# Attention, a dense layer and routed experts on one Trainium2 core: fourteen subtractions of the first dense unit moved from VectorE to GpSimd, one activation moved up

## The chip, the cores and the metric

The kernel runs on one core of one Trainium2 chip. The metric is the device time of one execution in microseconds; smaller is better. Before the change, three runs took 1003.2, 1003.36 and 1005.94 us, a median of 1003.36 us.

## What is computed

Attention with a learned bias over positions feeds a dense two-layer block, whose result feeds eight experts of which each token takes one:

```
x = attention(q, k, v, bias)            # 2304 tokens x 512
h = x @ w_in                            # 512 x 2048
g = h - tanh(h)
y = g @ w_out                           # 2048 x 512
e = argmax(y @ w_gate)                  # one of 8 experts per token
out = gate * (relu(y @ w1[e]) @ w2[e])
```

Only the dense block (the middle three lines) is touched by the change.

## The kernel before, in words

All matrix products of the dense block are made from pairs of numbers. Each operand is kept as a high part (rounded) and a low part (the value less its high part), and every product is three matmuls: high by high, high by low, low by high. ScalarE writes the high part (a copy with rounding), and VectorE the low part (a subtraction of the high part from the value, both in SBUF).

The dense block walks over six units of 384 tokens (`Moe1`, `u` from 0 to 5). In a unit, each of 16 blocks `m` of the hidden layer goes through

- `l1(u, m)`: 12 matmuls of 128x384 (line 795) into one of two PSUM buffers `h`;
- `act(u, m)`: g = h - tanh(h), where tanh(h) is near h by a polynomial. ScalarE makes `z`, `t`, `mk` and `v` (lines 807, 808, 810, 811, 812), VectorE makes `w` from them (lines 813, 814, 817, 818, 819). Lines 813 and 814 read `h` from PSUM; 814 is the last reader of that buffer, so that `l1` of block m+2 waits for it. Lines 817, 818 and 819 read SBUF alone. There is one mask buffer `mk`: line 810 of a block waits for line 819 of the block before;
- `split_g(u, m)`: high part `gh` on ScalarE (line 825), low part `gl` on VectorE (line 826), both from SBUF;
- `l2(u, m)`: 9 matmuls of 128x512 (line 839) into three accumulators `y`, three steps after `l1`.

The order on each engine is the order of the program text, which the function `experts` writes step by step (step `i` is block `m` of a unit): `l1` of block i, `l2` of block i-3, then `stage.at`, then `act` of block i, then `split_g` of block i-1.

`stage.at` is where weights and tokens are brought in. Of the 32 weight blocks (16 of the first layer, "which" 0, and 16 of the second, "which" 1), 14 are split during attention by `high_w`; the other 18 are brought in during the first dense unit: `w_job` loads a block into one of four buffers `raw` (line 741, SP's queue) and `split_w` makes its high part (line 747, ScalarE) and its low part (line 749, VectorE). Ten of those 18 are of the second layer (blocks 6 to 15), eight of the first (blocks 8 to 15). They come at steps 1 (two), 2, 3, 4, 5 (two), 6, 7, 8, 9 (two), 10, 11, 12, 13 (two) and 14. In the same buffers come the four pieces of the next unit's tokens (`x_job`, at steps 7, 9, 11 and 13): the load, a scaling on GpSimd (line 774), the high part on ScalarE (line 779) and the low part on VectorE (line 783). A buffer `raw` is free for the load of the fourth job behind it once the low part is made.

Of the kernel before, what the change touches and what calls it, by code (L numbers as in the profile page):

```python
# [17 lines left out]
ALU = mybir.AluOpType  # L18
# [12 lines left out]
def r32(ap):  # L31
    return ap.bitcast(F32R)
# [656 lines left out]
class Moe1:  # L689
# [52 lines left out]

        return load, lambda: self.split_w(which, m, st.pop("raw"))

    def high_w(self, which, m, raw):
        nc, t = self.tc.nc, self.weights.tile(f"w{which}_{m}")
        nc.scalar.activation(r32(t[:, 0, :]), raw, AF.Copy)
        (self.win, self.wout)[which][m] = t
        return lambda: nc.vector.tensor_tensor(r32(t[:, 1, :]), raw, t[:, 0, :], op=ALU.subtract)

    def split_w(self, which, m, raw):
        self.high_w(which, m, raw)()

    def x_tiles(self, u):

# [3 lines left out]
    def x_job(self, u, k):  # L759
        nc, n, st = self.tc.nc, self.N, {}  # L760

        def load():
            st["raw"] = self.stage.raw(f"xf{u}_{k}")
            st["r"] = self.weights.first.tile([128, n], F32, name=f"xr{u}_{k}", tag="xr", bufs=2)
            t = slice(n * u, n * u + n)
            nc.sync.dma_start(st["raw"][:, 0:n], self.xt_d[128 * k : 128 * k + 128, t])
            for b in range(n * u // S, (n * u + n - 1) // S + 1):
                a, z = max(n * u, S * b), min(n * u + n, S * b + S)
                for j in range(2):
                    r = self.r_d[k, b, j : j + 1, a - S * b : z - S * b].to_broadcast([64, z - a])  # L770
                    nc.sync.dma_start(st["r"][64 * j : 64 * j + 64, a - n * u : z - n * u], r)

        def scale():
            nc.gpsimd.tensor_tensor(st["raw"][:, 0:n], st["raw"][:, 0:n], st.pop("r"), op=ALU.mult)

        def high():
            if k == 0:
                self.x[u] = self.x_tiles(u)
            nc.scalar.activation(r32(self.x[u][0][:, k, :]), st["raw"][:, 0:n], AF.Copy)

        def low():
            h, l = self.x[u]
            nc.vector.tensor_tensor(r32(l[:, k, :]), st.pop("raw")[:, 0:n], h[:, k, :], op=ALU.subtract)

        return load, scale, high, low

# [605 lines left out]
def experts(moe1, moe2, router, stage):  # L1392

    tc = moe2.tc
    nc = tc.nc
    nu, ns = Moe1.NU, 2 * (EARLY + FIXED)
    e0 = 16 * nu  # L1400
    items = [("m", u, m) for u in range(nu) for m in range(16)]
    items += [("e", s, f) for s in range(ns) for f in range(8)]
    first = {"m": moe1.l1, "e": moe2.l1}
    act = {"m": moe1.act, "e": moe2.act}
    second = {"m": moe1.l2, "e": moe2.l2}
    plan = {}

    def at(i, f, *a):
        plan.setdefault(i, []).append(lambda: f(*a))

    routed = [16 * u + 15 + LAG + (12 if u + 1 < nu else 10) for u in range(nu)]
    known = []
    for k in range(EARLY):
        i = routed[nu - 1 - EARLY + k] + 1 + 2 * k
        at(i, router.early, k)
        at(i + 2, moe2.early_regs, k)
        known.append(i + 3)
    i = routed[-1] + 1
    for j, f in enumerate(router.table()):
        at(i + j - 1, f)  # L1420
    for k in range(FIXED):
        at(i + 3, moe2.table_regs, EARLY + k, k)
        known.append(i + 4)
    at(i + 3, moe2.table_regs, ("s", 0), FIXED)
    for s in range(ns):
        b = e0 + 8 * s
        at(max(known[s // 2], b - 15), moe2.ids, s)
        for t in range(3):
            at(max(known[s // 2] + 2, b - 12), moe2.gather, s, t)
            at(b - 8 + t, moe2.x_in, s, t)  # L1430
            if s < ns - 1:
                at(b + 8 + LAG + t, moe2.out_t, s, t)
            else:
                at(b + 8 + LAG, moe2.out_t, s, t, ("tr", "y0", "y1")[t])
    for p in range(ns // 2):
        b = e0 + 16 * p
        for n in range(16):
            stage.add(START + max(known[p] + 3, b - 10) + (9 * n) // 10, START + max(known[p], b - 16), *moe2.w_job(p, n))
    b = e0 + 8 * ns
    at(b + LAG, moe2.small_l2, 0)  # L1440
    at(b - 20, moe2.small_ids, 0)
    for n in range(8):
        at(b - 16 + n, moe2.small_w, 0, n)
    at(b - 6, moe2.small_gather, 0)
    at(b - 2, moe2.small_x, 0)
    at(b - 1, moe2.small_l1, 0)
    at(b + 1, moe2.small_t, 0)

    split = None
    for i in range(len(items) + LAG):  # L1450
        if i < len(items):
            kind, *a = items[i]
            if i > 1:
                first[kind](*a)
        if i >= LAG:
            y, *b = items[i - LAG]
            second[y](*b)
            if y == "m" and b[1] == 15:
                for d, f in enumerate(router.unit(b[0], [moe1.acc.pop((b[0], t)) for t in range(3)])):
                    if f:  # L1460
                        at(i + 1 + d, f)
            elif y == "e" and b[1] == 7:
                moe2.y_out(b[0])
        if i < 2:
            moe1.split_g(0, i)
        stage.at(START + i)
        if 1 < i < len(items):
            act[kind](*a)
        if split:
            moe1.split_g(*split)  # L1470
        split = a if 1 < i < len(items) and kind == "m" else None
        for f in plan.pop(i, ()):
            f()
    for i in sorted(plan):
        for f in plan[i]:
            f()

    rest = nc.values_load(router.tab[0:1, 2 * NTAB : 2 * NTAB + 1], min_val=0, max_val=NREST)
    with tc.For_i(0, rest) as k:
        moe2.listed_regs(EARLY + FIXED, k + FIXED + 1)  # L1480
        moe2.pair(EARLY + FIXED)
# [3 lines left out]
def attention_moe(ctx, tc, q, k, v, moe_w_in, moe_w_out, w_gate, e_w1, e_w2, rows, dist, out):  # L1485
# [74 lines left out]
    router.open(pool, psum)  # L1560
    moe2 = Moe2(tc, pool, stage, moe1, psum, e_w1, e_w2, x2_d, list_d, out, router, ident)
    experts(moe1, moe2, router, stage)


# [35 lines left out]
```

## Time and profile before

| | |
|---|---|
| median of three runs | 1003.36 us |
| the profiled execution | 1004.94 us |
| its span, first to last instruction | 1003.1 us |
| TensorE busy (matmul) | 971.5 us, 97% |
| VectorE busy | 760.0 us, 76% |
| ScalarE busy | 633.2 us, 63% |
| GpSimd busy | 355.5 us, 35% |

The profiled execution is one run, 1.58 us above the median; 1.84 us of it lie outside the span. Busy shares are means over stages: the first dense unit, in which all that is changed lies, takes the span from 334 to 402 us, and its own rows have to be read. In the rows below, PE is TensorE's matmul, PEld its weight load, DVE is VectorE, ACT ScalarE, POOL GpSimd and SPq the queue of DMA issues on SyncE.

### The profile page before, as it was taken

Reading aid. Unit: us, or ns where it says so; the run is one execution under the profiler, and the core shown is the slowest. Engines: PE = TensorE matmul, PEld = TensorE weight load, DVE = VectorE, ACT = ScalarE, POOL = GpSimd, SP = SyncE. Lnnn points to the kernel's source line nnn. Section 1 sums busy time; section 2 is a strip of 40 time slices with the busy share of each in tenths; the row PEclk is TensorE's granted clock in tenths of the full one; section 3 lists DMA queues with packets and bytes.
Section 4 is the critical chain, followed back from the end, with each engine's and each line's share of the span. In section 5 each row is a group of like instructions: output and inputs, shape, how many; then the busy total and the mean of one; then the engine's idle time right before and its main releaser. Section 6 shows DMA issues by size and latency. Waiting matters only on the chain.

```text
span 1003.1 us, 20010 instructions
## 1 busy us (share of the span) xinstructions
PE 971.5 (97%) x7091; PEld 818.4 (82%) x7091; DVE 760.0 (76%) x1739; ACT 633.2 (63%) x1469; POOL 355.5 (35%) x338
## 2 busy tenths in 40 slices
PE   7799999999999999999999999999999999999996
PEld 3467766666676798889888889888889999999995
DVE  8996788989989799889889888988896454434321
ACT  7797778778777788756666665666875433434321
POOL 9682889788788000100201101101121142222101
PEclk9999999999999999999999999999999999999999
DMA  8676586966954232300300300202223244433601
GB/s 245 210 196 204 158 225 181 254 180 162 260 165 135 73 99 84 94 3 1 95 1 1 95 1 13 84 1 74 67 77 106 86 116 140 131 112 122 212 19 35
DMA packets 112796, 113.28 MB, mean 113 GB/s; under 512 B 61795, under 2 KB 79715, under 8 KB 112692
## 3 DMA queue, kind: packets, MB, share of 16 engines
q1 hardware_dynamic: 107684, 99.96, 34.2%
q0 software_dynamic: 4864, 11.89, 3.8%
q8 instruction: 58, 0.95, 0.4%
q14 instruction: 46, 0.38, 0.1%
q10 hardware_dynamic: 144, 0.11, 0.0%
HBM read 81.90 MB, written 30.08 MB: 112 GB/s over the span
## 4 chain that ended last, share of the span: by engine, by line
PE 65%; DVE 14%; issue 10%; DMA 5%; ACT 3%; POOL 1%; SPq 1%; POOLq 0%; DVEq 0%; ACTq 0%
PE y L839 17%; PE h L795 17%; PE eh L1233 6%; PE ey L1255 6%; DVE p L306 4%; PE s L286 4%; PE px L380 4%; DVE hid L101 2%; PE pv L412 2%; PE bps L116 2%; DMA out<-o,id 2%; PE pv L439 2%; DVE pt L384 1%; PE tr L966 1%; DVE wc L633 1%
## 5 line engine op out<-in xcount | busy, mean ns | idle before, releaser
L795 PE MATMUL h<-xh,w 128*128 128x384 f32 x768 | 215.2, 341 | 2.1 <-DVE t L814 2.1
L839 PE MATMUL y<-w,gh 128*128 128x512 f32 x576 | 179.9, 393 | 0.0
L795 PEld LDWEIGHTS h<-xh,w 128*128 128x128 f32 x768 | 140.4, 188 | 8.3 <-DVE t L814 2.8
L320 ACT ACTIVATE p<-p,nm 128x576 f32<-128x576 f32 x144 | 111.3, 773 | 34.2 <-DVE nm L306 33.9
L795 PE MATMUL h<-xl,w 128*128 128x384 f32 x384 | 129.0, 336 | 0.0
L839 PEld LDWEIGHTS y<-w,gh 128*128 128x128 f32 x576 | 106.8, 188 | 17.1
L306 DVE CUSTOM_DVE_ANT_0 p<-s,bias 128x576 f32<-128x576 f32 x144 | 103.6, 751 | 19.8 <-PE s L286 18.3
L1233 PE MATMUL eh<-xh,ew 128*128 128x288 f32 x512 | 116.5, 303 | 0.0
L839 PE MATMUL y<-w,gl 128*128 128x512 f32 x288 | 113.8, 395 | 0.0
L1255 PE MATMUL ey<-ehh,ew 128*128 128x288 f32 x512 | 112.3, 295 | 0.0
L1243 DVE SCALAR_TENSOR_TENSOR ehl<-eh,ehh 128x288 fp32r<-128x288 f32 x64 | 29.2, 456 | 109.1 <-ACT ehh L1242 109.1
L1242 ACT ACTIVATE ehh<-eh 128x288 fp32r<-128x288 f32 x64 | 26.2, 410 | 124.2 <-PE ey L1255 122.9
L807 ACT ACTIVATE z<-h 128x384 f32<-128x384 f32 x96 | 46.5, 484 | 75.3 <-PE h L795 75.3
L1233 PEld LDWEIGHTS eh<-xh,ew 128*128 128x128 f32 x512 | 85.9, 189 | 0.3 <-issue 0.2
L380 PE MATMUL px<-ident,p 128*128 128x128 f32 x576 | 80.1, 281 | 6.2 <-DVE pt L384 2.8
L1255 PEld LDWEIGHTS ey<-ehh,ew 128*128 128x128 f32 x512 | 85.7, 189 | 0.4 <-issue 0.4
L380 PEld LDWEIGHTS px<-ident,p 128*128 128x128 f32 x576 | 62.0, 141 | 29.0 <-issue 12.5
L1272 POOL DMA_INDIRECT out<-o,id x24 | 22.9, 954 | 154.8 <-ACT o L1289 131.3
L1233 PE MATMUL eh<-xl,ew 128*128 128x288 f32 x256 | 75.6, 295 | 0.0
L1255 PE MATMUL ey<-ehl,ew 128*128 128x288 f32 x256 | 75.5, 295 | 0.0
L813 DVE SCALAR_TENSOR_TENSOR w<-z,h 128x384 f32<-128x384 f32 x96 | 53.0, 552 | 28.9 <-ACT t L808 26.3
L795 PEld LDWEIGHTS h<-xl,w 128*128 128x128 f32 x384 | 72.3, 188 | 2.4
(487 smaller groups left out, 2364.3 us busy)
## 6 DMA issues: line engine op xcount, KB each, us to landing
rw<-in_moe_w SPq DMA_DIRECT2D x64, 256.0 KB, 2.9
bias_d<-bo SPq DMA_DIRECT2D x36, 295.5 KB, 4.0
w<-in_moe_w_out SPq DMA_DIRECT2D x16, 512.0 KB, 3.6
w<-in_moe_w_in SPq DMA_DIRECT2D x16, 512.0 KB, 4.4
bias<-bias_d SPq DMA_DIRECT2D x16, 288.0 KB, 3.9
w_d<-wc SPq DMA_DIRECT2D x18, 256.0 KB, 2.6
xf<-xt_d SPq DMA_DIRECT2D x24, 192.0 KB, 5.1
raw<-w_d SPq DMA_DIRECT2D x18, 256.0 KB, 3.7
```

Of the source, the lines that this page charges most:

```text
L286: nc.tensor.matmul(ps[w][:, c, 0:288], r32(q[r, a, 128 * i : 128 * i + 128] if i < 4 else self.tails(u)[:, a, :]), r32(k[r, b, kc : kc + 2 ...
L306: nc.vector.tensor_tensor_reduce(st["p"][:, c].rearrange("p (a x) -> p a x", a=2), st["ps", w][:, :, 0:288], bias[:, c].rearrange("p (a x) ...
L320: nc.scalar.activation(p[:, c], p[:, c], AF.Exp, bias=nm[:, w : w + 1], scale=-1.0, accum_out=self.st[us[0], "sm"][:, x : x + 1])
L380: nc.tensor.transpose(ps[:, 128 * j : 128 * j + 128], p[:, 128 * n : 128 * n + 128], self.ident)
L795: nc.tensor.matmul(ps[:, 0 : self.N], a, r32(b[:, k, :]), start=k + i == 0, stop=k == 3 and i == 2)
L807: nc.scalar.activation(z, h, AF.Square)
L813: nc.vector.scalar_tensor_tensor(w, z, self.C4, h, op0=ALU.mult, op1=ALU.mult)
L839: nc.tensor.matmul(self.acc[u, t], r32(a[:, c]), r32(w[:, b, :]), start=m + i == 0, stop=m == 15 and i == 2)
L1233: nc.tensor.matmul(ps[:, 0:SLOT], a, r32(b[:, k, 0:SLOT]), start=k + i == 0, stop=k == 3 and i == 2)
L1242: nc.scalar.activation(r32(h), ps[:, 0:SLOT], AF.Relu)
L1243: nc.vector.scalar_tensor_tensor(r32(l), ps[:, 0:SLOT], 0.0, h, op0=ALU.max, op1=ALU.subtract)
L1255: nc.tensor.matmul(st["y", d][:, 0:SLOT], a, r32(b), start=f + i == 0, stop=f == 7 and i == 2)
```

## The change

Three edits. The low part of a second-layer weight block that is brought in by `split_w` is made on GpSimd (the 14 blocks that `high_w` makes during attention stay on VectorE, and so do the eight first-layer blocks). The low part of each of the four token pieces of unit 1 is made on GpSimd; the pieces of all other units stay. At step 2, `act` stands ahead of `stage.at`.

```diff
-    def high_w(self, which, m, raw):
+    def high_w(self, which, m, raw, low=None):
         nc, t = self.tc.nc, self.weights.tile(f"w{which}_{m}")
         nc.scalar.activation(r32(t[:, 0, :]), raw, AF.Copy)
         (self.win, self.wout)[which][m] = t
-        return lambda: nc.vector.tensor_tensor(r32(t[:, 1, :]), raw, t[:, 0, :], op=ALU.subtract)
+        return lambda: (low or nc.vector).tensor_tensor(r32(t[:, 1, :]), raw, t[:, 0, :], op=ALU.subtract)
 
     def split_w(self, which, m, raw):
-        self.high_w(which, m, raw)()
+        self.high_w(which, m, raw, self.tc.nc.gpsimd if which else None)()
...
         def low():
             h, l = self.x[u]
-            nc.vector.tensor_tensor(r32(l[:, k, :]), st.pop("raw")[:, 0:n], h[:, k, :], op=ALU.subtract)
+            e = nc.gpsimd if u == 1 else nc.vector
+            e.tensor_tensor(r32(l[:, k, :]), st.pop("raw")[:, 0:n], h[:, k, :], op=ALU.subtract)
...
         if i < 2:
             moe1.split_g(0, i)
+        if i == 2:
+            act[kind](*a)
         stage.at(START + i)
-        if 1 < i < len(items):
+        if 2 < i < len(items):
             act[kind](*a)
```

Below, numbers at the end of a name count buffers; `w_6` to `w_15` beside `raw` are weight blocks, `w_2_...` beside `z` and `v` is the activation of block 2.

VectorE at steps 1 to 3, before the change:

```order
L826 TENSOR_TENSOR gl_0_5299<-w_0_5241,gh_0_5298 128x384
L826 TENSOR_TENSOR gl_1_5303<-w_1_5262,gh_1_5302 128x384
L749 TENSOR_TENSOR w_6_5306<-raw_5087,w_6_5306 128x512
L749 TENSOR_TENSOR w_8_5309<-raw_5089,w_8_5309 128x512
L749 TENSOR_TENSOR w_7_5329<-raw_5091,w_7_5329 128x512
L813 SCALAR_TENSOR_TENSOR w_2_5337<-z_2_5334,h_2_5316 128x384
L814 TENSOR_TENSOR t_2_5336<-h_2_5316,t_2_5336 128x384
L817 SCALAR_TENSOR_TENSOR v_2_5335<-z_2_5334,v_2_5335 128x384
L818 SCALAR_TENSOR_TENSOR w_2_5337<-v_2_5335,w_2_5337 128x384
L819 COPY_PREDICATED w_2_5337<-mk_2_5338,t_2_5336 128x384
L749 TENSOR_TENSOR w_9_5374<-raw_5093,w_9_5374 128x512
```

The same place with the change (lines from 814 on stand one or more further down in the new text):

```order
L827 TENSOR_TENSOR gl_0_5299<-w_0_5241,gh_0_5298 128x384
L827 TENSOR_TENSOR gl_1_5303<-w_1_5262,gh_1_5302 128x384
L749 TENSOR_TENSOR w_8_5309<-raw_5089,w_8_5309 128x512
L814 SCALAR_TENSOR_TENSOR w_2_5332<-z_2_5329,h_2_5316 128x384
L815 TENSOR_TENSOR t_2_5331<-h_2_5316,t_2_5331 128x384
L818 SCALAR_TENSOR_TENSOR v_2_5330<-z_2_5329,v_2_5330 128x384
L819 SCALAR_TENSOR_TENSOR w_2_5332<-v_2_5330,w_2_5332 128x384
L820 COPY_PREDICATED w_2_5332<-mk_2_5333,t_2_5331 128x384
L749 TENSOR_TENSOR w_9_5374<-raw_5093,w_9_5374 128x512
```

Two of three weight subtractions ahead of the activation of block 2 are gone from VectorE; the one of the first-layer block 8 (step 1) still stands ahead of it, since the activation was moved past the split of step 2 alone.

GpSimd through the unit, as a piece of the difference (lines with + are new; line 784 is the old 783):

```order
 L734 MEMSET cst 128x1
+L749 TENSOR_TENSOR w_6_5306<-raw_5087,w_6_5306 128x512
+L749 TENSOR_TENSOR w_7_5344<-raw_5091,w_7_5344 128x512
+L749 TENSOR_TENSOR w_8_5420<-raw_5312,w_8_5420 128x512
+L749 TENSOR_TENSOR w_9_5469<-raw_5347,w_9_5469 128x512
 L774 TENSOR_TENSOR xf_0_5472<-xf_0_5472,xr_0_5473 128x384
+L749 TENSOR_TENSOR w_10_5569<-raw_5423,w_10_5569 128x512
+L784 TENSOR_TENSOR xl_5573<-xf_0_5472,xh_5572 128x384
 L774 TENSOR_TENSOR xf_1_5578<-xf_1_5578,xr_1_5579 128x384
+L749 TENSOR_TENSOR w_11_5673<-raw_5526,w_11_5673 128x512
+L784 TENSOR_TENSOR xl_5573<-xf_1_5578,xh_5572 128x384
 L774 TENSOR_TENSOR xf_2_5683<-xf_2_5683,xr_2_5684 128x384
```

GpSimd had four instructions of any length in this unit, the scalings of line 774; now it has eighteen, and each low part of a token piece stands ahead of the next piece's scaling in its queue.

## Rows read from the trace of the kernel before

**Rows 1.** The page: span, and busy time of each engine.
```profile
span 1003.1 us, 20010 instructions
PE 971.5 (97%) x7091; PEld 818.4 (82%) x7091; DVE 760.0 (76%) x1739; ACT 633.2 (63%) x1469; POOL 355.5 (35%) x338
```
**Rows 2.** Chain that ended last, in order of time: start us, us, work.
```profile
402.40 2.08 PE h L795 x12
...
406.58 2.08 PE h L795 x12
...
753.45 2.08 PE y L839 x9
```
**Rows 3.** Timeline of PE, 345 to 403 us: start, us, instruction, [idle before <-releaser].
```profile
349.94 0.45 PE L795 MATMUL h<-xh,w 128*128 128x384 f32 x1 [0.88 <-DVE t L814]
...
380.06 0.44 PE L795 MATMUL h<-xh,w 128*128 128x384 f32 x1 [0.58 <-DVE t L814]
...
397.98 0.42 PE L795 MATMUL h<-xh,w 128*128 128x384 f32 x1 [0.65 <-DVE t L814]
...
402.24 0.34 PE L795 MATMUL h<-xh,w 128*128 128x384 f32 x1
```
**Rows 4.** Timeline of DVE, steps 2 and 6 of the unit, and its end.
```profile
347.05 1.90 DVE L749 TENSOR_TENSOR w<-raw,w 128x512 fp32r<-128x512 f32 x3
348.87 0.55 DVE L813 SCALAR_TENSOR_TENSOR w<-z,h 128x384 f32<-128x384 f32 x1
349.33 0.55 DVE L814 TENSOR_TENSOR t<-h,t 128x384 f32<-128x384 f32 x1
...
362.73 0.56 DVE L818 SCALAR_TENSOR_TENSOR w<-v,w 128x384 f32<-128x384 f32 x1
...
400.47 0.55 DVE L813 SCALAR_TENSOR_TENSOR w<-z,h 128x384 f32<-128x384 f32 x1
```
**Rows 5.** Timeline of ACT, steps 3, 4 and 6.
```profile
352.38 0.62 ACT L810 ACTIVATE mk<-z,cst 128x384 f32<-128x384 f32 x1 [0.63 <-DVE w L819]
...
356.07 0.62 ACT L810 ACTIVATE mk<-z,cst 128x384 f32<-128x384 f32 x1 [0.22 <-DVE w L819]
...
362.13 0.62 ACT L747 ACTIVATE w<-raw 128x512 fp32r<-128x512 f32 x1
```
**Rows 6.** Timeline of DVE at the four scalings of POOL in the unit.
```profile
366.43 1.26 DVE L818 SCALAR_TENSOR_TENSOR w<-v,w 128x384 f32<-128x384 f32 x1
...
374.95 1.37 DVE L818 SCALAR_TENSOR_TENSOR w<-v,w 128x384 f32<-128x384 f32 x1
...
383.60 1.39 DVE L817 SCALAR_TENSOR_TENSOR v<-z,v 128x384 f32<-128x384 f32 x1
...
392.86 1.28 DVE L818 SCALAR_TENSOR_TENSOR w<-v,w 128x384 f32<-128x384 f32 x1
```
**Rows 7.** Timeline of POOL, the second and fourth scaling of the unit.
```profile
374.89 1.02 POOL L774 TENSOR_TENSOR xf<-xf,xr 128x384 f32<-128x384 f32 x1 [7.62 <-DMA xr<-r_d]
...
392.71 1.02 POOL L774 TENSOR_TENSOR xf<-xf,xr 128x384 f32<-128x384 f32 x1 [8.13 <-DMA xr<-r_d]
```
**Rows 8.** One line, its instructions (ns min/median/max): two kinds of two-input work on POOL.
```profile
L774 POOL TENSOR_TENSOR xf<-xf,xr x24: 997/1023/1419, 162.1 to 638.0; 128x384 f32<-128x384 f32 x24
L628 POOL TENSOR_TENSOR w<-w x32: 1037/1039/1078, 103.7 to 323.8; 128x512 int32<-128x512 int32 x32
```
**Rows 9.** Timelines of POOL and DVE at 498 us, third unit.
```profile
498.26 1.42 POOL L774 TENSOR_TENSOR xf<-xf,xr 128x384 f32<-128x384 f32 x1 [2.09 <-DMA xr<-r_d]
...
498.91 0.56 DVE L813 SCALAR_TENSOR_TENSOR w<-z,h 128x384 f32<-128x384 f32 x1
499.38 0.55 DVE L814 TENSOR_TENSOR t<-h,t 128x384 f32<-128x384 f32 x1
```
**Rows 10.** Timelines of DVE and SPq around the last token piece; waits, 345 to 402 us.
```profile
387.18 0.56 DVE L783 TENSOR_TENSOR xl<-xf,xh 128x384 fp32r<-128x384 f32 x1
...
387.76 0.33 SPq L766 DMA_DIRECT2D xf<-xt_d  x1
...
ACT xh L779 <- POOL xf L774: 0.7, 2, 0.6
```

## The prediction

> **What bounds the kernel now.** I began with the page's busy row: TensorE is busy 97% of the span [rows 1]. A change can therefore help only where TensorE idles, and hurts wherever it makes TensorE idle. The chain of waits comes next: from 402 to 753 us it is matmuls, an h block every 4.18 us (402.40 to 406.58) [rows 2]. That part starts when the first unit is done, so any time that the first unit gains or loses goes to the end of the kernel one for one.
>
> Then TensorE's timeline of the first unit. It stops three times for more than half a microsecond, each time for line 814 on VectorE [rows 3], the last reader of the PSUM buffer that the next h block needs. What is there to win can be bounded. From 349.94 to 402.24 are twelve steps, 52.30 us [rows 3]; at 4.18 us they would take 50.16. So 2.14 us are lost there, and 0.88 more just ahead of 349.94 [rows 3]. **The most this change can gain is 3.0 us**, which is also about what a measurement of this kernel can tell from no change (0.3%).
>
> Why is VectorE late? Two limits lie close together. One is a loop between two engines: the mask of a block waits for the last instruction of the block before, and through lines 810, 811, 812 on ScalarE and 817, 818, 819 on VectorE the next mask follows. It took 3.69 us from 352.38 to 356.07, both ends released by line 819 [rows 5]. That is 0.49 us under TensorE's 4.18. The other is VectorE's own work: from 348.87 to 400.47, twelve steps, it took 51.60 us, 4.30 a step [rows 4], against 4.18.
>
> **What the edits take away.** Three weight subtractions in a row go from 347.05 to 348.87, 0.61 us each [rows 4]. Ten leave VectorE: 6.1 us. Four token subtractions leave it too; the step between such instructions of 384 columns is 0.46 us (348.87 to 349.33 [rows 4]): 1.8 us. By that alone VectorE would need some 3.6 us a step, the loop's 3.69 would be the bound, TensorE would never wait, and all 3.0 us would be won.
>
> **What they add.** Fourteen GpSimd instructions with two SBUF inputs. GpSimd has four of that sort in this unit already, the scalings, so the price can be read off. Beside each, one VectorE instruction that reads two SBUF operands is stretched from 0.56 us to 1.26, 1.37, 1.39 and 1.28 us [rows 6], against 0.56 for its undisturbed like [rows 4]. That is 0.70, 0.81, 0.83 and 0.72 us, 0.77 in the mean, for a GpSimd instruction of 1.02 us [rows 7]: VectorE starts only when GpSimd is nearly done. So a moved subtraction saves VectorE 0.46 us (token piece) and can cost it 0.77.
>
> The Trainium skill (Perfetto Trace Analysis, Optimizing Scalar/DVE Operations) speaks against the change: since the two engines share an SBUF read port, moving work between them may not help. By it the gain of the last paragraph but one would be given back; by the rows it is more than given back, for the reason that follows.
>
> A weight subtraction has 512 columns, and no row shows one on GpSimd. The bounds: not under the integer addition of 512 columns, 1.04 us, and not over the longest scaling drawn out to 512 columns, 1.42 x 4/3 = 1.89 us [rows 8]. Nearest is the usual scaling, same type and two inputs, drawn out: 1.02 x 4/3 = 1.36 us [rows 8]. So it should stretch a VectorE instruction by 0.77 + 0.34 = 1.11 us (bounds 0.79 and 1.64) and saves 0.61. The Trainium skill (GPSIMD Engine Reference, Elementwise: side-by-side cycle accounting) has a two-input addition of 2048 columns at 4497 ns; a quarter of it, an estimate, is 1.12 us, and the stretch would be 0.87, which would take about 1.9 us off the sum below. No row of this case shows which is nearer.
>
> **Where they land.** The high part of a weight block is made on ScalarE at 362.13 to 362.75 while VectorE enters line 818 (362.73) [rows 4, 5]. GpSimd can start there, and line 819 stands behind it, which closes the loop. Not all land so: lines 813 and 814 read PSUM, and they were not stretched beside a scaling that ran from 498.26 to 499.68 (0.56 and 0.55 us) [rows 9]. They take 0.93 of a step's 3.69 us, a quarter.
>
> **The sum**, over the twelve steps from the activation of block 2 to that of block 14. The loop: 12 x 3.69 = 44.3 us; what VectorE has left (five instructions of an activation, the low part of g, at most one weight block) fits beside it. GpSimd work in these steps: nine weight blocks (7 to 15; block 6 comes before), 9 x 1.11 = 10.0; four scalings, 4 x 0.77 = 3.1; four token pieces, right behind a weight block in GpSimd's queue, where VectorE has had its turn and is likely on lines 813 and 814: half price, 4 x 0.39 = 1.6. Together 14.7 us. With all of it on the loop: 59.0 us against 51.6, 7.4 us later. With a quarter of it beside lines 813 and 814: 55.3, 3.7 us later. I take 5.4, between the two: some fall in the free quarter, but a step that is faster than TensorE saves nothing for a later one, since it has two PSUM buffers and waits.
>
> **The third activation.** It passes one split out of three; one more is off VectorE in any case, and one (first-layer block 8) still stands ahead. Without the port, line 814 would come two subtractions earlier, 1.2 us, and the stall of 0.88 us would go. But GpSimd's first weight block starts when its high part is ready, at about the 347.05 us at which VectorE took it [rows 4], and holds up the subtraction behind it by about 0.6 us, with 0.5 us of wait for that block's own high part. So I count 0.2 us of gain. On ScalarE the split's copy moves behind the five instructions of `act` and delays nothing that is due: its block is used six steps later.
>
> Costed at nothing: DMA issues, which are the same in number and order; the second layer's matmuls, whose weights are split at least four steps (16 us) before use; later units, whose own instructions don't change.
>
> **Sum: 5.4 - 0.2 = 5.2 us later.** For the profiled execution that is 1004.94 + 5.2 = 1010.1 us; its runs' median stands 1.58 lower, so the median goes from 1003.36 to **1008.6 us**. With the bounds of the 512-column price (9 x 0.79 or 9 x 1.64 in place of 10.0, at the same share) the sum runs from about 2.7 to 9.3.
>
> **The rivals.**
> *The port costs nothing that counts* (ends on the other side). If GpSimd's instructions fell where VectorE waits or reads PSUM, VectorE would be relieved of 7.9 us, the loop's 3.69 us would hold against 4.18, and all stalls go: 1003.36 - 3.0 = 1000.3 us, at the edge of what can be told. It decides from the point where a step's stretch is below 0.49 us. For it: VectorE will have gaps that it has not now. Against it: four scalings out of four stretched VectorE in this unit [rows 6], and the high part comes ready just ahead of line 819. Chance 0.06.
> *A draw.* Five of the nine weight blocks and the scalings land on the loop, the rest beside PSUM readers: 44.3 + 5.6 + 3.1 = 53.0, 1.4 later, less the 0.2: 1004.6 us. Chance 0.22.
> *GpSimd's queue becomes late as well.* The load of the fourth token piece is issued at 387.76 us, as soon as the low part of the third (387.18) has freed its buffer, and its scaling runs 5 us later, at 392.71 [rows 7, 10]. ScalarE waits for scalings already, 0.7 us in two waits [rows 10], and z and t of the next activation are queued behind that wait. If the low parts, now behind a weight block of 1.36 us and slower themselves, free the buffers 1.5 us later in each of the two last rounds, some 3 us come on top: 5.2 + 3 = 8.2, 1011.6 us. Chance 0.14.
> *The change does less than its words say*: it does so at the third activation, and the sum has it.
> The forecast itself: 0.58.
>
> **How the numbers follow.** Forecast and late queue are slower by over 3.0 us: 0.72. The draw is the same: 0.22. Free port: I count it as faster, 0.06, though it lies at the edge. The likeliest case alone runs from 1006.4 to 1010.8. The range of 8 in 10 leaves out the free port, a corner of the draw and the end of the late queue: 1002.0 to 1012.0.
>
> **What would show it.** If I am right, the number of stretched lines 817, 818, 819 and 826 in the first unit rises from four to ten or more, at 1.3 us (scalings) and up to 1.7 us (weight blocks); GpSimd's 512-column instructions take 1.1 to 1.9 us; TensorE's idle time before line 795 for line 815 (the old 814) grows from 2 us to 6 or more; the first h block of unit 1 starts at about 407 us in place of 402.24; and from there to the end nothing changes but the offset. I am wrong if that block starts before 402 us, if stretched instructions are mostly ones that nobody waits for, or if the shift at 407 us is not found again at the end.

## The result, and the profile after

Seven runs of each kernel give these medians: 1009.41 us with the change (1008.24 to 1012.33), 1003.48 us before (1002.34 to 1006.44). The measured ratio is 1.0053 with a 95% interval of 1.0041 to 1.0065 (the medians alone divide to 1.0059): slower, by a little more than the 0.3% that a measurement of this kernel can tell. The forecast was 1008.6 us, in a range of 1002.0 to 1012.0. The profiled execution took 1010.16 us (forecast 1010.1), its span 1008.4.

The page of the changed kernel, span and busy row, to be set beside [rows 1]:

```profile
span 1008.4 us, 20010 instructions
...
PE 971.0 (96%) x7091; PEld 817.7 (81%) x7091; DVE 763.6 (76%) x1725; ACT 633.3 (63%) x1469; POOL 375.4 (37%) x352
```

VectorE has fourteen instructions fewer (1725 for 1739) and is busy 3.6 us longer (763.6 for 760.0). That is the result in one line: work left the engine, and what stayed on it became slower by more.

TensorE's timeline of the first unit in the changed kernel, all its stops from step 2 on and the start of unit 1 (columns as in [rows 3]):

```profile
349.70 0.45 PE L796 MATMUL h<-xh,w 128*128 128x384 f32 x1 [0.87 <-DVE t L815]
...
357.82 0.50 PE L840 MATMUL y<-w,gl 128*128 128x512 f32 x1 [0.75 <-DVE gl L827]
...
362.61 0.51 PE L840 MATMUL y<-w,gl 128*128 128x512 f32 x1 [0.34 <-DVE gl L827]
...
372.19 0.50 PE L840 MATMUL y<-w,gl 128*128 128x512 f32 x1 [0.95 <-DVE gl L827]
...
381.39 0.50 PE L840 MATMUL y<-w,gl 128*128 128x512 f32 x1 [0.57 <-DVE gl L827]
...
390.68 0.50 PE L840 MATMUL y<-w,gl 128*128 128x512 f32 x1 [0.67 <-DVE gl L827]
...
400.80 0.50 PE L840 MATMUL y<-w,gl 128*128 128x512 f32 x1 [1.48 <-DVE gl L827]
...
403.25 0.41 PE L796 MATMUL h<-xh,w 128*128 128x384 f32 x1 [0.56 <-DVE t L815]
...
407.50 0.34 PE L796 MATMUL h<-xh,w 128*128 128x384 f32 x1
```

Unit 1 starts at 407.50 us, where it started at 402.24 [rows 3]; from there to the end of the span it is 600.9 us in both (1008.4 - 407.50 and 1003.1 - 402.24). So the loss lies in the first unit and goes to the end one for one. The first h block of unit 0, in the kernel before and with the change:

```profile
334.41 0.45 PE L795 MATMUL h<-xh,w 128*128 128x384 f32 x1
334.19 0.44 PE L796 MATMUL h<-xh,w 128*128 128x384 f32 x1
```

From here on **the stage** is the time from the first h block of unit 0 to the first of unit 1: 67.83 us before (334.41 to 402.24), 73.31 with the change (334.19 to 407.50), 5.48 more.

The stops are of a new kind. Before, TensorE waited ahead of line 795 for the last reader of PSUM [rows 3]. Now six of its eight stops lie in the second layer's matmuls, for the low part of g (line 827). The waits of the changed kernel, 345 to 412 us (engine, tile and line, releaser: us in total, times, longest):

```profile
ACT mk L811 <- DVE w L820: 12.9, 12, 2.4
...
PE y L840 <- DVE gl L827: 4.8, 6, 1.5
...
PE h L796 <- DVE t L815: 1.4, 2, 0.9
```

TensorE's waits come to 6.2 us, where they were 2.1 [rows 3], and none of them is for GpSimd. That is 4.1 us more, for a stage that is 5.48 longer. The rest is what a stop costs beyond its named wait: the matmul at 372.19 us starts 1.12 us behind the pace of the step before it, of which 0.95 is named, and the one after it 1.23 us behind. Five stops more, at about 0.28 us each (an estimate from that stop and the one at 400.80), make up the other 1.4 us.

Why the low part? One step shows it. Here are timelines of the changed kernel around 369 us, of GpSimd, VectorE and ScalarE (columns as in [rows 4, 5, 7]):

```profile
367.21 1.02 POOL L774 TENSOR_TENSOR xf<-xf,xr 128x384 f32<-128x384 f32 x1 [5.08 <-DMA xr<-r_d]
368.67 1.29 POOL L749 TENSOR_TENSOR w<-raw,w 128x512 fp32r<-128x512 f32 x1 [0.44 <-DVE v L818]
369.92 1.33 POOL L784 TENSOR_TENSOR xl<-xf,xh 128x384 fp32r<-128x384 f32 x1
...
367.20 0.55 DVE L815 TENSOR_TENSOR t<-h,t 128x384 f32<-128x384 f32 x1
367.69 0.96 DVE L818 SCALAR_TENSOR_TENSOR v<-z,v 128x384 f32<-128x384 f32 x1
368.69 1.69 DVE L819 SCALAR_TENSOR_TENSOR w<-v,w 128x384 f32<-128x384 f32 x1
370.41 1.29 DVE L820 COPY_PREDICATED w<-mk,t 128x384 f32<-128x384 int32 x1
371.60 0.54 DVE L827 TENSOR_TENSOR gl<-w,gh 128x384 fp32r<-128x384 f32 x1
...
371.79 0.62 ACT L811 ACTIVATE mk<-z,cst 128x384 f32<-128x384 f32 x1 [2.04 <-DVE w L820]
```

Three GpSimd instructions follow one another, and three VectorE instructions in a row take 0.96, 1.69 and 1.29 us where their undisturbed like take about 0.56 to 0.61. The mask on ScalarE waits 2.04 us for the last of them, and the low part of g behind them is ready at 372.14; TensorE's matmul that reads it starts at 372.19, after its 0.95 us of idle time in the fence above. Lines 818, 819, 820 and 827 all stand between line 815, which lets the first layer go on, and the end of the low part, which lets the second layer go on. Undisturbed that way takes 2.1 us (362.23 to 364.37 us in the kernel before); TensorE has 2.08 us of first-layer matmuls [rows 2] and about half a microsecond of second-layer ones (370.61 to 371.07 at its pace) before it needs the result. That leaves about 0.4 us, and one instruction stretched by 1.1 us uses up more.

Seventeen VectorE instructions from 347 to 404 us are stretched, where there were four [rows 6]. I set each beside the GpSimd instruction that it runs against and took off its undisturbed duration (0.55 to 0.61 us, 0.68 for a weight subtraction). The table has those that fall into the prediction's twelve steps:

| GpSimd work in the twelve steps | forecast | measured |
|---|---|---|
| nine weight blocks | 9 x 1.11 = 10.0 us | 8.6 us (0.96 to 1.13 each; the last, mostly beside PSUM readers, 0.27) |
| four scalings | 4 x 0.77 = 3.1 us | 1.4 us (0.40; 0, beside PSUM readers; 0.27; 0.69) |
| four token pieces | 4 x 0.39 = 1.6 us | 3.0 us (0.69, 0.83, 0.68, 0.82) |
| together | 14.7 us | 13.0 us |

### The profile page after: what moved, and what is told of

It is laid out like the page before. It is cut to its first block, busy times and chain, and to the rows that moved or that the text cites. A ratio compares the mean times of both kernels' runs of the same rounds, so it can differ in the third digit from the quotient of the medians.

```text
span 1008.4 us, 20010 instructions
## 1 busy us (share of the span) xinstructions
PE 971.0 (96%) x7091; PEld 817.7 (81%) x7091; DVE 763.6 (76%) x1725; ACT 633.3 (63%) x1469; POOL 375.4 (37%) x352
## 4 chain that ended last, share of the span: by engine, by line
PE 66%; DVE 16%; issue 8%; DMA 5%; ACT 3%; SPq 1%; POOL 0%; DVEq 0%; POOLq 0%; ACTq 0%
PE y L840 17%; PE h L796 17%; PE eh L1234 8%; PE ey L1256 7%; DVE p L306 4%; PE s L286 4%; PE px L380 4%; DVE hid L101 3%; PE pv L412 2%; PE pv L439 2%; DVE pt L384 1%; DMA out<-o,id 1%; PE bps L116 1%; DMA xt_d<-x 1%; DVE w L819 1%
## 5 line engine op out<-in xcount | busy, mean ns | idle before, releaser
L380 PEld LDWEIGHTS px<-ident,p 128*128 128x128 f32 x576 | 62.1, 141 | 29.0 <-issue 12.7
```

The source lines that it names most:

```text
L380: nc.tensor.transpose(ps[:, 128 * j : 128 * j + 128], p[:, 128 * n : 128 * n + 128], self.ident)
```

## The experiments

The runs below were made in three groups (e1 to e4; e5 to e8; e9, e10 and e1b), each on one chip and beside the kernel before, which took 1007.83, 1007.13 and 1006.85 us there. The stage of the kernel before and of the change is that of the section above. Attention ahead of the stage ended up to 4 us apart in the profiles of these kernels, so what is compared first is the stage, and the time beside it. A stage is read from one profiled execution; the same kernel twice (e1, e1b) gave stages 0.19 us apart.

| kernel | stage, us | its ends, us | time / before, interval |
|---|---|---|---|
| before | 67.83 | 334.41, 402.24 | |
| the change | 73.31 | 334.19, 407.50 | 1.0053, 1.0041 to 1.0065 |
| e1, activation of block 2 alone | 67.22 | 336.34, 403.56 | 0.9986, 0.9975 to 0.9997 |
| e1b, the same again | 67.41 | 335.90, 403.31 | 0.9997, 0.9987 to 1.0006 |
| e2, ten weight subtractions alone | 72.99 | 333.00, 405.99 | 1.0038, 1.0026 to 1.0051 |
| e3, four token subtractions alone | 69.09 | 334.06, 403.15 | 1.0009, 0.9998 to 1.0020 |
| e4, all fourteen left out | 65.25 | 334.29, 399.54 | 1.0995 (see there) |
| e7, the same, another low part read | 65.23 | 332.90, 398.13 | 1.0031, 1.0014 to 1.0047 |
| e5, memsets in their place | 65.26 | 335.04, 400.30 | 1.0034, 1.0020 to 1.0048 |
| e10, copies in their place | 66.20 | 334.65, 400.85 | 1.0058, 1.0043 to 1.0074 |
| e6, GpSimd held back | 71.91 | 335.64, 407.55 | 1.0040, 1.0028 to 1.0053 |
| e8, scalings on VectorE, one step early | 72.79 | 335.15, 407.94 | 1.0057, 1.0040 to 1.0075 |
| e9, scalings on VectorE, in their place | 66.68 | 332.58, 399.26 | 0.9989, 0.9980 to 0.9998 |

The theory: a GpSimd instruction with two inputs in SBUF holds up VectorE's two-input SBUF instructions for nearly as long as it lasts. The rivals are three. GpSimd's queue makes transfers late, whatever it does there; or the place of the GpSimd work in the step is what hurts; or the low parts that GpSimd makes arrive late at TensorE.

### Which part of the change costs

**e1**, the activation alone:

```diff
+        if i == 2:
+            act[kind](*a)
         stage.at(START + i)
-        if 1 < i < len(items):
+        if 2 < i < len(items):
```

> Theory (shared port): the loss comes from GpSimd instructions that hold up VectorE; moving the activation of block 2 ahead of one split takes about 0.6 us off the first stall of 0.88 us, and the first h block of unit 1 starts 0 to 0.6 us earlier than in the kernel before; the time is 0 to 0.6 us less, which the median can hardly tell. Rival (the moved activation is the loss, because the splits behind it come late): 2 us or more slower than before, with TensorE waiting for weights. Rival (late queue): the same as the theory.

**e2**, the weight subtractions alone:

```diff
...
     def split_w(self, which, m, raw):
-        self.high_w(which, m, raw)()
+        self.high_w(which, m, raw, self.tc.nc.gpsimd if which else None)()
```

> Only the ten weight subtractions go to GpSimd. Theory (shared port): they make about two thirds of the stretch (8.6 of 13 us in the changed kernel), so the first h block of unit 1 starts 3 to 5 us later than before, and the time is 3 to 5 us longer. Rival (late queue: the token pieces' low parts wait in GpSimd's queue and free their buffers late): with the token pieces back on VectorE the loss goes to 1.5 us or less. Rival (moved activation): no loss, since it is not moved here.

**e3**, the token pieces alone:

```diff
...
+            e = nc.gpsimd if u == 1 else nc.vector
+            e.tensor_tensor(r32(l[:, k, :]), st.pop("raw")[:, 0:n], h[:, k, :], op=ALU.subtract)
```

> Only the four token subtractions go to GpSimd. Theory (shared port): four stretches of 0.7 to 0.8 us against 0.46 saved each, on top of a unit in which VectorE is the bound: 0.5 to 2 us longer than before. Rival (late queue): most of the loss is here, 3 us or more. Rival (moved activation): no change.

Against the stage of 67.83 us they give -0.61, +5.16 and +1.26 us: 5.81 together, where the whole change gives 5.48. The weight blocks are nearly all of it; e2 lies just above the 3 to 5 us that were expected. The third rival does not fit here: in the stage of the change, of e2 and of e3, no wait of TensorE is for GpSimd, neither of its matmuls nor of its weight loads.

In e1 the stop ahead of block 4's first layer fell from 0.88 us [rows 3] to 0.34; in the whole change it stayed at 0.87. The reason is in VectorE's timeline. With the change:

```profile
347.35 1.37 DVE L749 TENSOR_TENSOR w<-raw,w 128x512 fp32r<-128x512 f32 x1 [0.48 <-ACT w L747]
348.64 0.54 DVE L814 SCALAR_TENSOR_TENSOR w<-z,h 128x384 f32<-128x384 f32 x1
```

and in e1, where nothing runs on GpSimd there:

```profile
348.98 1.29 DVE L749 TENSOR_TENSOR w<-raw,w 128x512 fp32r<-128x512 f32 x2
350.25 0.56 DVE L813 SCALAR_TENSOR_TENSOR w<-z,h 128x384 f32<-128x384 f32 x1
```

One subtraction beside GpSimd's (1.37 us, with 0.48 of wait ahead of it) lasts longer than the two that VectorE makes by itself (1.29 us). **e1b** ran the same kernel as e1 in more rounds:

> The activation of block 2 moved up and nothing else, once more and in more rounds. If its gain is real: a stage of 67.0 to 67.4 us and a time of 0.9980 to 0.9995 of the kernel before. If it was scatter: a ratio whose interval lies around 1.000.

The stage came out 0.42 us shorter than before, just above the range that was expected; the time, at 0.9997, cannot be told from no change, and by the test set ahead of the run a gain in time is not shown. In the stage, moving the activation is worth about half a microsecond and no more (0.61 and 0.42).

### What could be won, and what GpSimd's reading costs

**e4** leaves the fourteen subtractions out (not asked for in `split_w` and in the token pieces' `low`):

```diff
...
+            parts = ((gh, 0), (gh, int(m < 6)), (gl, 0))
...
+        xl = xh if u == 1 else xl
```

> The changed kernel without its fourteen subtractions at all (those low parts are left out, and the matmuls that would read them read the high parts instead, so TensorE does the same work). This is what the change would give if GpSimd's work cost nobody anything. All theories: TensorE's stalls of the first unit go but for the first, 1.5 to 3.2 us less than the kernel before, 1000.3 to 1002 us, and only the four scalings stretch VectorE. If it is no faster than before, VectorE's load was not what TensorE waited for, and the loop between ScalarE and VectorE is.

The stage was 65.25 us, 2.58 less than before; the forecast's bound on what could be won was 3.0. The total, 1.0995, says nothing about the change: with high parts read twice the values are others, the tokens went to other experts, and the expert stage grew (640 matmuls of the line that is 1233 in the kernel before, for 512). So **e7** leaves out the same and reads another block's low part, which is small:

```diff
...
+            parts = ((gh, w, 0), (gh, w if m < 6 else self.wout[0], 1), (gl, w, 0))
...
+                b = self.wout[0][:, 1, 0 : self.N] if u == 1 and i == 1 else b[:, k, :]
```

> The kernel of e4 again, with the matmuls that would read the missing low parts reading another small low part in place of the high part, so that the values stay near the reference's and the tokens go to the same experts. All theories: the dense stage takes 65.3 us as in e4 (67.83 before), and the time is 2 to 3 us less than the kernel before. A time far above it as in e4 would mean that the routing was not the reason there.

The stage is 65.23 us, as in e4. The time, which was expected to be 2 to 3 us less than before, is 1.0031 of it; what is known of that follows below. **e5** is e7 with two memsets on GpSimd where each subtraction would be:

```diff
...
+            self.tc.nc.gpsimd.memset(raw, 0.0)
+            self.tc.nc.gpsimd.memset(raw, 0.0)
```

> The changed kernel with each of its fourteen GpSimd subtractions replaced by two GpSimd memsets of the same width over the raw buffer, which wait for the same high part and free the same buffer (some 1.1 us of GpSimd work that writes SBUF and reads nothing); the low parts are left out, and the matmuls that would read them read another small low part. Theory (shared port, as a matter of what GpSimd reads): VectorE is not stretched, and the dense stage from the first h block of unit 0 to the first of unit 1 takes about 65.3 us, as in the kernel with the subtractions left out. Variant (any GpSimd access to SBUF holds VectorE up): stretches of 0.4 us or more at lines 818, 819, 820 and 827, and 70 to 73 us. Rival (late queue): GpSimd is as long busy and frees the buffers about as late, so a good part of the 73.3 us of the changed kernel stays, 68 us or more, without stretches.

And **e10** is e7 with a copy, which reads one operand:

```diff
...
+            self.tc.nc.gpsimd.tensor_copy(raw, raw)
```

> The fourteen low parts are left out (another small low part is read in their place), and GpSimd copies each buffer onto itself where the low part would be made: one input from SBUF, in place of the two of the subtraction or the none of the memset. Theory (what holds VectorE up is that GpSimd reads SBUF): lines 818, 819, 820 and 827 are stretched by nearly the duration of the copy, and the stage is 66.5 to 71 us, against 65.2 with the work left out or with memsets and 73.3 with the subtractions. Rival (only GpSimd's second input contends): no stretched instruction beside a copy and a stage of 65.0 to 65.6 us.

Groups of GpSimd's instructions in the stage (count, busy us, mean ns, idle time and what ended it), in e5:

```profile
L755 POOL MEMSET raw<- 128x512 f32 x10 | 5.3, 527 | 0.6
L754 POOL MEMSET raw<- 128x512 f32 x10 | 5.3, 526 | 28.8 <-ACT w L747 28.8
L779 POOL TENSOR_TENSOR xf<-xf,xr 128x384 f32<-128x384 f32 x4 | 5.2, 1298 | 20.7 <-DMA xr<-r_d 10.2 <-DVE v L828 5.4 <-DVE t L825 5.0
```

in e10:

```profile
L754 POOL COPY raw<-raw 128x512 f32<-128x512 f32 x10 | 6.9, 696 | 32.0 <-ACT w L747 28.1 <-issue 4.0
```

and in e2, as a measure of the subtraction:

```profile
L749 POOL TENSOR_TENSOR w<-raw,w 128x512 fp32r<-128x512 f32 x10 | 14.7, 1476 | 30.1 <-ACT w L747 30.1
```

A pair of memsets keeps GpSimd at work for 1.05 us a block, close to one subtraction of 1.28 to 1.32, and the stage is 65.26 us: nothing is lost against leaving all out. So it is not that GpSimd's queue is busy, and not that the buffers come free later. VectorE's groups in e5 are undisturbed but for the four scalings, for instance line 837, the low part of g:

```profile
L837 DVE TENSOR_TENSOR gl<-w,gh 128x384 fp32r<-128x384 f32 x14 | 7.6, 546 | 0.2 <-ACT gh L836 0.2
```

With the copies, VectorE's timeline in e10 has stretched lines again, and the stretches are shorter (lines 827, 828 and 835 there are 819, 820 and 827 of the change); first GpSimd's copies of 512 columns, then VectorE beside them:

```profile
350.78 0.61 POOL L754 COPY raw<-raw 128x512 f32<-128x512 f32 x1 [2.84 <-ACT w L747]
355.37 0.62 POOL L754 COPY raw<-raw 128x512 f32<-128x512 f32 x1 [3.97 <-issue]
359.89 0.69 POOL L754 COPY raw<-raw 128x512 f32<-128x512 f32 x1 [3.91 <-ACT w L747]
...
350.82 0.98 DVE L827 SCALAR_TENSOR_TENSOR w<-v,w 128x384 f32<-128x384 f32 x1
355.53 0.92 DVE L828 COPY_PREDICATED w<-mk,t 128x384 f32<-128x384 int32 x1
360.04 0.95 DVE L835 TENSOR_TENSOR gl<-w,gh 128x384 fp32r<-128x384 f32 x1
```

A copy of 0.61 us costs VectorE 0.98 - 0.56 = 0.42 us, a subtraction of 1.29 us 1.68 - 0.56 = 1.12 (the block at 350.33 us of the change), a memset nothing. The other two copies above cost 0.32 and 0.40 us, the blocks at 355.55 and 360.73 us of the change (1.32 and 1.41 us on GpSimd) 0.96 and 1.10. What decides is that GpSimd reads SBUF, and the price, where VectorE comes to such an instruction just behind GpSimd's start, is GpSimd's duration less 0.2 to 0.4 us. The Trainium skill (SBUF — State Buffer, SBUF: two separate sides) has the pair of ports that both engines share as an exclusive lock, which a VectorE instruction with two SBUF inputs needs only against a GpSimd instruction that reads SBUF. All three runs agree with that, and so do lines 814 and 815, which read PSUM and stay at 0.55 us (means of 548 and 550 ns in the whole stage of the change).

The stage of e10, 66.20 us, lies under the 66.5 that the theory expected. 0.4 us more in a step is still less than the 0.49 that the loop has to spare in it, which would explain why only about 1 us shows; this was not tested by itself.

In e5, e7 and e10 the total is 1.003 to 1.006 of the kernel before though the stage is shorter. Some 5.6 us are lost some 370 us later, in the expert stage: from the start of unit 1 to the last matmul of line 1233 (by its number before) they take 585.0 us, e1 and the kernel before 579.4. TensorE's timeline of e7:

```profile
767.38 0.87 PE L1224 MATMUL ext<-ident,xg 96*128 96x96 f32 x4 [4.18 <-issue]
```

e5 and e10 have the same gap of 4.18 us, no other kernel of the table has it (e4, whose expert stage is another, left aside), and units 1 to 5 are as long as elsewhere. These three read another block's low part; why the expert stage then stops there stays open. It is why their stage is read and not their time.

### The place in the step

**e6** holds GpSimd back: ahead of each moved subtraction, from step 3 on, a copy of one column waits for the low part of g of the step but one before, so that GpSimd starts behind the lines that close the loop.

```diff
...
+    def gate(self):
+        if self.step is not None and self.step >= 3:
+            gl = self.g[0, self.step - 2][1]
+            self.tc.nc.gpsimd.tensor_copy(self.cst[:, 3:4], gl[:, 0:1])
...
```

> The changed kernel, with a copy of one column ahead of each moved subtraction on GpSimd from step 3 on, which waits for VectorE's low part of g of the step but one before (line 827), so that the same work starts a little later, when VectorE comes to the two instructions that read PSUM. Theory (shared port): the price depends on what VectorE does beside it; stretches of lines 819 and 820 become rarer, and the dense stage falls from 73.3 to 69 to 71.5 us. Rival (late queue): all of GpSimd's work is later, so the stage is as long or longer, 73 us or more.

The stage is 71.91 us: 1.40 less than the change, 4.08 more than before, and a little above the 69 to 71.5 that were expected. Groups of VectorE in e6, from 345 to 404 us, with the three lines that close the loop (820, 819 and 827 of the change):

```profile
L830 DVE COPY_PREDICATED w<-mk,t 128x384 f32<-128x384 int32 x12 | 8.0, 663 | 0.4
L829 DVE SCALAR_TENSOR_TENSOR w<-v,w 128x384 f32<-128x384 f32 x12 | 7.8, 652 | 0.4
L837 DVE TENSOR_TENSOR gl<-w,gh 128x384 fp32r<-128x384 f32 x12 | 7.4, 616 | 0.2 <-ACT gh L836 0.2
```

and the same in the change, from 345 to 404 us too:

```profile
L820 DVE COPY_PREDICATED w<-mk,t 128x384 f32<-128x384 int32 x12 | 11.6, 964 | 0.4
L819 DVE SCALAR_TENSOR_TENSOR w<-v,w 128x384 f32<-128x384 f32 x13 | 11.2, 861 | 0.5
L827 DVE TENSOR_TENSOR gl<-w,gh 128x384 fp32r<-128x384 f32 x12 | 9.5, 792 | 0.2 <-ACT gh L826 0.2
```

Most of the stretch is gone (663, 652 and 616 ns for 964, 861 and 792; over the twelve steps 4.2 us are left of 13.0) and most of the loss is not. What came in its place stands in the waits of e6, 345 to 412 us:

```profile
ACT xh L787 <- POOL xf L782: 7.0, 4, 2.3
...
DVE w L824 <- ACT t L819: 4.8, 3, 2.3
```

GpSimd's queue, which now waits for VectorE, is late with the scalings; ScalarE waits 7.0 us for them where it waited 0.7 [rows 10], z and t of the next activation stand behind that wait, and VectorE waits 4.8 us for t. So the rival on the place is half right: the place decides how much is stretched, and this place, which stretches less, costs a wait. How the 4.08 us divide between that wait and the stretch that is left was not separated.

### Turning it round: the scalings to VectorE

If GpSimd's reading is dear and VectorE's own 0.46 us a 384-column instruction is cheap, the four scalings that GpSimd makes in this unit should gain by going the other way. Both kernels below are e1 with that.

**e8** scales on VectorE at the end of steps 6, 8, 10 and 12, one step earlier than the split of before, which moves one step back:

```diff
...
+            e = nc.vector if u == 1 else nc.gpsimd
...
+    for k, f in enumerate(moe1.mid):
+        at(6 + 2 * k, f)
```

> The opposite step, from the kernel before: the activation of block 2 ahead of its split (e1), and the four scalings of unit 1's token pieces moved from GpSimd to VectorE, one step ahead of their high parts, the pieces' splits one step later. Theory (shared port): each scaling costs VectorE 0.46 us of its own in place of a stretch of 0.77; the unit has no stretched instruction left, the dense stage takes 66.0 to 66.9 us (67.22 in e1, 67.83 before), and the time is 1 to 2 us less than the kernel before. Rival (VectorE is the bound by its own instruction count alone): 1.8 us of work more on VectorE, the stage longer than in e1, 68 us or more.

It missed: 72.79 us. No line of VectorE is stretched, but its queue stands still ahead of the scalings for 6.8 us, of which 4.7 are put down to a load and 2.1 to nothing that the profile shows. Groups of VectorE in e8 (the last numbers are the idle time ahead of them and what ended it):

```profile
L824 DVE COPY_PREDICATED w<-mk,t 128x384 f32<-128x384 int32 x12 | 7.3, 606 | 0.4
...
L779 DVE TENSOR_TENSOR xf<-xf,xr 128x384 f32<-128x384 f32 x4 | 2.2, 557 | 6.8 <-DMA xr<-r_d 4.7 <-issue 2.1
```

**e9** scales at the step at which the piece was split before (7, 9, 11 and 13), and splits it at the end of that step:

```diff
...
+                    if u == 1:
+                        self.mid.append(split)
+                        both, split = load, scale
...
+            e = nc.vector if u == 1 else nc.gpsimd
...
+    for k, f in enumerate(moe1.mid):
+        at(7 + 2 * k, f)
```

> The fourteen low parts stay on VectorE, the activation of block 2 is moved up, and the four scalings of unit 1 are made on VectorE at the step at which their pieces were split before, so that their load has had as long as it has now. Theory (a GpSimd instruction with two SBUF inputs costs VectorE about 0.75 us, the same work on VectorE 0.46): the four stretched instructions of the unit go (3.1 us) and 1.8 us of scalings come, so the stage from the first block of unit 0 to that of unit 1 is 66.0 to 67.0 us, against 67.8 of the kernel before and 67.2 with the activation alone; time 0.997 to 0.999 of the kernel before. Rival (VectorE's queue stands behind a load, as when the scaling came a step earlier): a stage of over 68 us, with a wait for the load of xr ahead of line 779.

The stage is 66.68 us, 1.15 less than before and within what was expected: the shortest here of the kernels that compute everything. The activation alone gave 0.61 and 0.42 of it (e1, e1b), so the scalings are worth 0.5 to 0.7 us. The time is 0.9989 of the kernel before (0.9980 to 0.9998), about 1.1 us; that is less than 0.3%, and it lies between the two measurements of the activation alone (0.9986 and 0.9997), so that the times do not rank them. VectorE's groups in e9:

```profile
L823 DVE COPY_PREDICATED w<-mk,t 128x384 f32<-128x384 int32 x14 | 8.4, 603 | 0.5
L822 DVE SCALAR_TENSOR_TENSOR w<-v,w 128x384 f32<-128x384 f32 x14 | 7.8, 558 | 0.5
...
L778 DVE TENSOR_TENSOR xf<-xf,xr 128x384 f32<-128x384 f32 x4 | 2.2, 554 | 0.9 <-DMA xr<-r_d 0.8
```

All lines are undisturbed, and the idle time ahead of the scalings is 0.9 us in place of 6.8. One stop of 0.87 us is left late in the stage, for a weight block's high part, and one of 0.34.

## Why the prediction was right, and where its steps were not

**What bounds the kernel** held: unit 1 to the end is the same 600.9 us, offset and all. **The most that can be won** was put at 3.0 us and measured at 2.58 to 2.60 (e4, e7). **That a moved subtraction costs VectorE more than it saves** held for both kinds: e2 and e3 are each longer than before, by 5.16 and 1.26 us.

**The sum** of 5.4 us came out at 5.38 (VectorE's first instruction of block 2 to that of block 14: 348.64 to 405.62 us, 56.98, for 51.60 [rows 4]). The second of these, with the change:

```profile
405.62 0.56 DVE L814 SCALAR_TENSOR_TENSOR w<-z,h 128x384 f32<-128x384 f32 x1
```

That is closer than its terms were. The stretches were put at 14.7 us and measured 13.0: the scalings at 3.1 and measured 1.4 (the second in the table stretched nothing, since VectorE was on lines 814 and 815, and the first and third about a half and a third of the 0.77 of [rows 6]); the weight blocks at 10.0 and measured 8.6, since 512 columns take GpSimd 1.28 to 1.32 us and not 1.36, and one block fell mostly beside PSUM readers; the token pieces at 1.6 and measured 3.0. **The half price of the token pieces is the step that was wrong in kind**: I had VectorE on lines 814 and 815 by then, but a VectorE instruction held up by a weight block ends about 0.4 us after that block, with the piece already at work, and the next one in the queue, line 820 or 827, meets it. They were at full price, four times. The share on the loop was wrong the other way: I took 12.7 of 14.7 us (57.0 - 44.3), a choice between two bounds and not worked out, and it is 12.7 of 13.0. Two misses cancel, and that the sum fits to 0.02 us is luck. That the stretches land on the loop is not: from the end of one line 820 to the next, the eleven steps from 352.67 to 405.08 us took 3.69 us and the stretches between, each within 0.05 us (3.70 with none, 5.91 with 0.40, 1.13 and 0.68). The waits say the same: the mask waited for line 820 in twelve steps (12.9 us).

The price of a 512-column subtraction lay nearest the row that was chosen, of the same kind and drawn out by columns. A quarter of the 2048-column figure of the Trainium skill (GPSIMD Engine Reference, Elementwise: side-by-side cycle accounting), an estimate of 1.12 us, is under the 1.28 to 1.32 us of the undisturbed instructions; the trace decides.

**The third activation** was put at 0.2 us of gain and brought 0.01 (0.87 for 0.88). Its two holds were as forecast (0.69 us of stretch, 0.48 of wait); only their sum against the 0.5 us that it brings by itself (e1: 0.88 to 0.34) was judged too kindly.

**Where TensorE would wait** was wrong. I named line 796 for line 815, 6 us or more; it was 1.4 us, and 4.8 at line 840 for the low part of g. The mechanism that makes VectorE late was right, but I followed the loop only to the mask, and not to its other reader: the stretched lines stand behind line 815 and ahead of line 827, so that the second layer is the first to notice. This did not change the sum. The other signs that I had named came: seventeen stretched instructions for ten or more, GpSimd's 512-column subtractions mostly at 1.3 to 1.6 us, unit 1 at 407.50 for 407, and the same offset at the end.

**The rivals.** A free port falls: e5 shows what free work on GpSimd would look like, and the subtractions are 8.05 us over it (73.31 - 65.26). The draw falls with the share on the loop. The late queue falls: e5 has a queue nearly as long (18.6 us of GpSimd's time in the stage for 23.2) and loses nothing, and with the change ScalarE waited for a scaling once in the whole kernel, 1.0 us, where it waited 1.7 us in three waits before.

## What to carry to other kernels

Before work is moved from VectorE to an idle GpSimd, look at what both read. Here a GpSimd subtraction or copy that reads SBUF held up a VectorE instruction with two SBUF inputs for its duration less 0.2 to 0.4 us, so that a subtraction of 0.61 us taken off VectorE could cost it 1.1 us, and it cost the path that VectorE is on, not GpSimd's. Work that only writes cost nothing (e5), and work that ran beside VectorE's PSUM readers little or nothing (the second scaling in the table), but the wait that moved it away from the loop ate most of what it saved (e6: 8.8 us less of stretch, a stage 1.40 us shorter). Ask for every engine that reads the stretched lines' results, not only for the one that waits now. That GpSimd was busy for only 35% of the span said nothing about what its work would cost another engine.

## What the runs showed of the hardware that was not expected

- Memsets on GpSimd neither stretch VectorE nor are held up by it: 526 and 527 ns for 128x512, twenty of them.
- GpSimd is held up too. Its subtractions take 1.28 us at best and 1476 ns in the mean of e2; two in a row took 3.15 us with the change. The scalings, 1.02 us by themselves, took 1298 ns in the mean of e5 (line 779 there). In the kernel before, the scaling of 1.42 us at 498.26 us [rows 9] started together with a VectorE subtraction of two SBUF operands, and there it was VectorE that kept its time:

```profile
498.26 0.55 DVE L826 TENSOR_TENSOR gl<-w,gh 128x384 fp32r<-128x384 f32 x1
```

- Three GpSimd instructions in a row stretched three VectorE instructions in a row (from 367.21 us on, in the timelines above): each VectorE instruction ended about 0.4 us after the GpSimd instruction beside it, and the next met the next.
- The same wait for a load is dear on one queue and cheap on the other. GpSimd stood idle for 7.62 and 8.13 us ahead of two of its scalings [rows 7], and ScalarE lost 0.7 us by it [rows 10]. On VectorE one step early the four left it idle for 6.8 us (e8, a stage of 72.79 us), and in their place for 0.9 us (e9, 66.68).
